# Value products per tile over four column tiles, placed beside each key tile, in a decode attention kernel

## The chip, the cores and the metric

One core of one Trainium2 chip. The metric is the device time of one execution in microseconds (us). Where a text says "span" it means the profiled execution from the first to the last instruction of the core. "Clock" is the share of its full speed that TensorE was granted; the clock records hold 1.0 and 0.5 ("half clock"), and between two changes lie 3.41 us or a multiple of it (3.41 to 40.96 us in the kernel before). A "stop" is idle time of TensorE that ended for no reason that the profile shows; the lines mark it `<-issue`. A run is called slow when it is over 1.5% above the fastest of the same kernel; medians are over all runs.

## The reference, cut to what matters

```python
# A: one decode step of attention, batch 4, 32 query heads on 8 key/value heads, head size 128, window 4096
q = (x @ wq).reshape(B, 1, 32, 128)
k = k_cache[:, :, -4096:, :]; v = v_cache[:, :, -4096:, :]      # each repeated 4 times over the query heads
p = softmax(q @ k^T * 128 ** -0.5)
a = (p @ v).reshape(B, 1, 4096) @ wo
# B: a small gated feed-forward of the same x;   g = sigmoid(sum(x * gate_w))
out = g * a + (1 - g) * b
```

Keys and values of the window are 67 MB of the 81 MB that are read. Everything else is small, so loading is the floor: the 81.01 MB of the page take 191 us at the 425 GB/s of its slices, an estimate.

## The kernel before

The cache is cut into 16 tiles of keys (`k 0..15`) and 16 of values (`v 0..15`), 2 MB each: one batch entry and two heads, called a pair. Two pairs make a set (8 sets). One queue on the sync engine issues all loads in a fixed order; keys have 4 slots and values 5. Per set TensorE transposes the key tiles (KT), multiplies by the queries (SC), exchanges row maxima (SW), transposes the exponentials (PT), sums rows (RS), multiplies by the values (PV), regroups the result (OQ) and at the end projects with `wo` (WO). Each engine is given its instructions in the order of this list:

```python
def _pe_order():
    ...
    for s in range(2, NSET):
        o += [("KT", 2 * s), ("PT", s - 1), ("KT", 2 * s + 1), ("SC", s), ("PV", s - 2), ("SW", s), ("RS", s - 2),
              ("OQ", s - 2)]
        if s == 6:
            o.append(("WO", 0))
    last = NSET - 1
    o += [("PV", last - 1), ("RS", last - 1), ("PT", last), ("RS", last), ("OQ", last - 1)]
    o += [("PVL", 0), ("OQL", 0), ("WO", 2), ("PVL", 1), ("OQL", 1), ("WO", 3)]
```

The value products of a set are 128 matrix products with 8 weight columns, alternating between the two pairs and two column tiles of each pair. "Column tile" is said here of the place that `pos` below gives to a product (0, 32, 64 or 96); its 8 rows of the result begin at that row of the bank. The last set is done pair by pair (PVL), so there only two of the four column tiles are in use:

```python
def pv_mm(s, pair, ch, ev=None, waits=()):
    c0 = 32 * (ch // 2) + 16 * pair + 8 * (ch % 2)
    r = 64 * pair + 32 * (ch % 2)                       # the column tile
    mm(banks[OB][r:r + 8, 0:128], pT[:, s % 2, c0:c0 + 8],
       Vsb[:, (2 * s + pair) % VSLOTS, 128 * ch:128 * ch + 128], ch < 2, ch > 61, ..., pos=(0, r))
...
w = [("PV", (i - VSLOTS) // 2)] if i >= VSLOTS else []   # a value load waits for the whole set that held its slot
...
def _kt_on_act(i, f):                                   # which of 8 blocks of a key tile ScalarE copies back
    return i % 2 == 1 and f % 2 == 1
```

## Time and profile before

| | before |
|---|---|
| timed median (3 runs) | 219.79 us (218.59 to 220.63) |
| span of the profiled run | 216.0 us |
| loads at about 425 GB/s | from 2.4 to 191.7 us, then a gap, last value piece at 202.77 us |
| last set's scores start, last exponentials end | 187.46, 198.92 us |
| TensorE busy, mean clock | 156.3 us (72%), 0.897 |

The part of the page that follows the chain of work back from the last instruction says how much of the span each engine and each line carried:

```profile
PE 40%; DMA 36%; ACT 10%; DVE 7%; issue 4%; SPq 2%; ACTq 0%; DVEq 0%
DMA Ksb<-in_A_k_cache_dram 29%; PE bank L327 26%; PE bank L331 14%; DMA Wbig<-in_A_wq_dram 8%; ACT Ksb L670 7%; ACT pe L693 2%; DVE Ksb L553 2%; DVE pe L585 2%; SPq L251 2%; DVE qblk L577 1%; DVE osb L620 1%; DVE pT L611 1%; DVE osum L656 0%; DVE hmax L604 0%; DVE negmax L606 0%
```

The reader should see that key loads carry 29% and all loads 36% of the chain: in the middle the engines wait for keys, and only the last part is a chain of engines. The prediction shows that part line by line.

### The profile page before, as it was taken

To read this page: it belongs to the slowest core of one execution; us is meant where nothing else is said; L and a number is where in the kernel's file an instruction comes from. 1 tells how busy PE (TensorE), PEld (TensorE's weight loads), DVE (VectorE), ACT (ScalarE), POOL (GpSimd) and SP (SyncE) were. 2 spreads that over 40 slices of the span, in tenths; PEclk is the share of its full clock that TensorE was granted. 3 is DMA by queue.
4 is the path that set the end of the run, shared out by engine and by line. 5 is a ranking of instruction groups with operands and counts; after the bars stand their busy time and mean duration, and the time that the engine had idled before them with its cause. 6 is when DMAs were issued, how large, how long until landed. Compare 5 with 4: busy or idle time off the path is not lost.

```text
span 216.0 us, 5261 instructions
## 1 busy us (share of the span) xinstructions
PE 156.3 (72%) x2398; PEld 109.2 (51%) x2398; DVE 114.0 (53%) x257; ACT 76.9 (36%) x70; POOL 3.4 (2%) x16
## 2 busy tenths in 40 slices
PE   0385917889991057889788788578778599785894
PEld 0382605367261055388277457545763347445751
DVE  3181682787575013569469559346785119561302
ACT  2000313287053015084446618151860720618000
POOL 6000000000000000000000000000000000000000
PEclk9996797999999558969999999799999879999569
DMA  5999999999999999999999999999999999818300
GB/s 200 444 425 410 428 426 423 439 429 420 425 396 415 433 431 428 425 428 425 425 428 422 428 434 419 425 425 423 432 428 419 419 425 434 376 58 271 124 0 1
DMA packets 6837, 81.33 MB, mean 377 GB/s; under 512 B 792, under 2 KB 800, under 8 KB 2336
## 3 DMA queue, kind: packets, MB, share of 16 engines
q1 hardware_dynamic: 6816, 81.01, 89.4%
q8 instruction: 18, 0.29, 0.6%
q14 instruction: 3, 0.02, 0.0%
HBM read 81.01 MB, written 0.00 MB: 375 GB/s over the span
## 4 chain that ended last, share of the span: by engine, by line
PE 40%; DMA 36%; ACT 10%; DVE 7%; issue 4%; SPq 2%; ACTq 0%; DVEq 0%
DMA Ksb<-in_A_k_cache_dram 29%; PE bank L327 26%; PE bank L331 14%; DMA Wbig<-in_A_wq_dram 8%; ACT Ksb L670 7%; ACT pe L693 2%; DVE Ksb L553 2%; DVE pe L585 2%; SPq L251 2%; DVE qblk L577 1%; DVE osb L620 1%; DVE pT L611 1%; DVE osum L656 0%; DVE hmax L604 0%; DVE negmax L606 0%
## 5 line engine op out<-in xcount | busy, mean ns | idle before, releaser
L331 PE MATMUL bank<-identf,Ksb 128*128 128x128 f32 x512 | 72.9, 304 | 28.1 <-DMA Ksb<-in_A_k_cache_dram 21.1
L331 PEld LDWEIGHTS bank<-identf,Ksb 128*128 128x128 f32 x512 | 65.3, 158 | 33.3 <-issue 12.9
L553 DVE COPY Ksb<-bank 128x1024 bf16<-128x1024 bf16 x96 | 61.5, 685 | 36.4 <-PE bank L331 36.1
L693 ACT ACTIVATE pe<-sc,negmax 64x2048 bf16<-64x2048 bf16 x16 | 41.6, 2601 | 52.8 <-DVE negmax L606 52.6
L670 ACT ACTIVATE Ksb<-bank 128x1024 bf16<-128x1024 bf16 x32 | 31.5, 1023 | 48.1 <-PE bank L331 48.0
L327 PE MATMUL bank<-Ksb,qblk 128*8 128x512 bf16 x256 | 30.8, 622 | 8.9 <-ACT Ksb L670 8.9
L595 DVE TENSOR_SCALAR_CACHE_REDUCE sc<-bank 128x512 bf16<-128x512 f32 x32 | 22.1, 692 | 21.3 <-PE bank L327 21.3
L327 PEld LDWEIGHTS bank<-Vsb,pT 128*8 128x8 bf16 x1024 | 19.1, 91 | 6.3 <-issue 6.3
L327 PE MATMUL bank<-Vsb,pT 128*8 128x128 bf16 x1024 | 20.8, 228 | 1.6 <-issue 1.1
L327 PEld LDWEIGHTS bank<-Ksb,qblk 128*8 128x8 bf16 x256 | 4.6, 88 | 29.2 <-DVE sc L595 13.4
L327 PE MATMUL bank<-sel,pe 128*128 128x32 bf16 x256 | 8.1, 178 | 6.7 <-ACT pe L693 6.6
L611 DVE CAST pT<-bank 128x512 bf16<-128x512 f32 x16 | 10.3, 682 | 3.3 <-PE bank L327 3.3
L327 PEld LDWEIGHTS bank<-sel,pe 128*128 128x128 bf16 x256 | 7.3, 97 | 8.2 <-DVE Ksb L553 5.9
L327 PE MATMUL bank<-Wbig,oq 128*4 128x512 bf16 x32 | 10.7, 500 | 0.7 <-DVE oq L640 0.7
L327 PE MATMUL bank<-oneh,osb 128*32 128x4 bf16 (+1 forms) x144 | 3.3, 176 | 7.0 <-DVE osb L620 5.0
L620 DVE TENSOR_SCALAR osb<-bank,recip 128x128 bf16<-128x128 f32 (+1 forms) x9 | 3.2, 351 | 8.7 <-PE bank L327 8.5
L327 PEld LDWEIGHTS bank<-oneh,osb 128*32 128x32 bf16 (+1 forms) x144 | 2.4, 115 | 8.1 <-DVE osb L620 6.0
L327 PEld LDWEIGHTS bank<-Wbig,oq 128*4 128x4 bf16 x32 | 3.0, 101 | 5.9 <-issue 3.5
L681 ACT ACTIVATE ge<-bank 4x1 f32<-4x1 f32 x2 | 0.2, 152 | 14.5 <-PE bank L327 14.5
L327 PE MATMUL bank<-Wbig,xT 128*4 128x512 bf16 x32 | 3.6, 625 | 2.2 <-DMA Wbig<-in_A_wq_dram 2.2
L604 DVE TENSOR_TENSOR hmax<-bank,rowmax 128x1 f32<-128x1 f32 x8 | 1.2, 156 | 7.4 <-PE bank L327 7.4
L585 DVE MEMSET pe<- 64x2048 bf16 x2 | 3.5, 1765 | 1.2 <-issue 1.2
(52 smaller groups left out, 48.3 us busy)
## 6 DMA issues: line engine op xcount, KB each, us to landing
Ksb<-in_A_k_cache_dram SPq DMA_DIRECT2D x16, 2048.0 KB, 25.3
Vsb<-in_A_v_cache_dram SPq DMA_DIRECT2D x15, 2048.0 KB, 25.5
Wbig<-in_A_wq_dram SPq DMA_DIRECT2D x1, 4096.0 KB, 16.3
Wbig<-in_A_wo_dram SPq DMA_DIRECT2D x1, 4096.0 KB, 31.0
Vsb<-in_A_v_cache_dram SPq DMA_DIRECT2D x4, 512.0 KB, 6.6
Vsb<-in_B_W_gate_dram SPq DMA_DIRECT2D x1, 1792.0 KB, 24.1
Vsb<-in_B_W_up_dram SPq DMA_DIRECT2D x1, 1792.0 KB, 33.3
Vsb<-in_B_W_down_dram SPq DMA_DIRECT2D x1, 1792.0 KB, 41.2
```

What stands on the lines that cost most here:

```text
L251: E.op(lambda: e.dma_start(dst, src), ev=ev, waits=waits, ctr=ctr)
L327: E.op(lambda: t.matmul(out_, lhsT, rhs, start=start, stop=stop, tile_position=pos, skip_group_check=True), ev=ev, waits=waits)
L331: E.op(lambda: t.transpose(out_, in_, idn), ev=ev, waits=waits)
L553: E.op(lambda: v.tensor_copy(kt_dst(i, f), bankb[tr(key)]), ev=("E",) + key, waits=[key])
L577: E.op(lambda r=r, u=u, b=b: v.tensor_copy(qv[r, b, n, :, :, :, u], src[r, :, :, b, :]), ev=("E",) + key if lastop else None, waits=[key, ...
L585: E.op(lambda n=n: v.memset(pev[64 * n:64 * n + 64, :, 1 - n], 0.0), ev=("PEZ",) if n else None, waits=[("QT", 1)])
L595: E.op(lambda: v.tensor_scalar(sc[:, 512 * f:512 * f + 512], banks[scb(key)], 1.0, None, op0=ALU.mult, op1=ALU.max, accum_out=mx4[:, f:f + ...
L604: E.op(lambda: v.tensor_tensor(hmax[:, :], banks[tr(key)][:, 0:1], rowmax[:, :], ALU.max), ev=("E",) + key, waits=[key])
L611: E.op(lambda: v.tensor_copy(pT[:, s % 2, 512 * f:512 * f + 512], banks[tr(key)]), ev=("E",) + key, waits=[key] + ([("PV", s - 2)] if s >= ...
L620: E.op(lambda: v.tensor_scalar(osb[r, s % 2, :], banks[OB][r, 0:128], recip[r, s % 2:s % 2 + 1], None, op0=ALU.mult), ev=ev, waits=waits)
L670: E.op(lambda: a.activation(kt_dst(i, f), bankb[tr(key)], ACTF.Copy), ev=("E",) + key, waits=[key])
L693: E.op(lambda r=r, n=n: a.activation(pev[r, :, n], sc[r, :], ACTF.Exp, bias=negmax[r, s % 2:s % 2 + 1], scale=SCALE, accum_out=rowsum[r, s ...
```

## The change

Its intent: do the value products one tile at a time, so that they fit into gaps beside each key tile, so that a value slot comes free per tile, and so that all four column tiles are used to the end. The core of the diff:

```diff
     for s in range(2, NSET):
-        o += [("KT", 2 * s), ("PT", s - 1), ("KT", 2 * s + 1), ("SC", s), ("PV", s - 2), ("SW", s), ("RS", s - 2),
-              ("OQ", s - 2)]
+        i = 2 * s
+        o += [("KT", i), ("OQ", i - 4), ("PT", s - 1), ("RS", s - 1)]
+        o += [("PV", i - 3), ("KT", i + 1)] if s < NSET - 1 else [("KT", i + 1), ("PV", i - 3)]
+        o += [("SC", s), ("OQ", i - 3), ("PV", i - 2), ("SW", s)]
         if s == 6:
             o.append(("WO", 0))
...
+    i = NPAIR - 4
+    o += [("OQ", i), ("PV", i + 1), ("PT", NSET - 1), ("OQ", i + 1), ("RS", NSET - 1), ("PV", i + 2), ("OQ", i + 2)]
+    o += [("WO", 1), ("PV", i + 3), ("OQ", i + 3), ("WO", 2)]
...
 # loads: "k 14, v 11, k 15, v 12 ..." becomes "k 14, k 15, v 11, v 12 ..."
...
-    return i % 2 == 1 and f % 2 == 1
+    return i % 2 == 1 and f in (1, 3, 6)
...
-                w = [("PV", (i - VSLOTS) // 2)] if i >= VSLOTS else []
+                w = [("PV", i - VSLOTS)] if i >= VSLOTS else []
...
+        def PV(i):
+            s, pair = i // 2, i % 2
...
+                r = 32 * (ch % 4)
+                c0 = 32 * (ch // 2) + 16 * pair + 8 * (ch % 2)
+                mm(banks[OB][r:r + 8, 0:128], pT[:, s % 2, c0:c0 + 8], Vsb[:, i % VSLOTS, 128 * ch:128 * ch + 128],
+                   ch < 4, ch > 59, ev=("PV", i) if ch == 63 else None, waits=w, pos=(0, r))
```

Row sums now need two products per set (one per pair), and norm, regrouping and its copy are done 16 times instead of 9. The rest of the diff is masks and names.

## The prediction

The packets in it are the 16 KiB ones of the instruction queue; the page of the kernel before lists 18. Two of its figures are estimates of its author: 27 ns for a value product over four column tiles at half clock, about half of the 56 ns over two (64 in 3.58 us), and 0.22 us for a projection at full clock, half of its 0.43 at half clock (8 in 3.51 us).

> **What bounds the kernel now.** I read the page's slices first, then the transfer queue's own timeline, then TensorE's timeline of the last third, then the chain that ended last. The slices (5.4 us each):
>
> ```profile
> PEclk9996797999999558969999999799999879999569
> DMA  5999999999999999999999999999999999818300
> GB/s 200 444 425 410 428 426 423 439 429 420 425 396 415 433 431 428 425 428 425 425 428 422 428 434 419 425 425 423 432 428 419 419 425 434 376 58 271 124 0 1
> ```
>
> To the reader: for 34 slices the DMA engines are full at about 425 GB/s, so up to about 190 us nothing that the engines do is worth anything unless it holds up a load. Then comes a hole (58 GB/s), a second piece of traffic, and about 13 us with no transfer at all. The gain is in those last slices. The hole has an owner in the queue's timeline (start us, us, queue, line, transfer, count):
>
> ```profile
> 150.50 0.61 SPq L251 DMA_DIRECT2D Ksb<-in_A_k_cache_dram  x1
> 151.14 45.04 SPq L251 DMA_DIRECT2D Vsb<-in_A_v_cache_dram  x7
> ```
>
> The last seven issues are value tiles 12, 13, 14 and the four pieces of 15; they stretch to 196 us because tile 15 may not be issued before its slot is given back. The landing records of the trace say: tile 14 complete at 191.70, pieces of tile 15 at 197.35 to 202.77. In the full stretch one 2 MB tile lands every 4.89 us, so without that wait tile 15 would be there at 191.7 + 4.9 = 196.6. But TensorE comes to tile 15's products only at 207.5, so the late load is not what ends the kernel. TensorE's timeline (start us, us, operation, count, idle before) shows what does:
>
> ```profile
> 166.30 1.98 PE L327 MATMUL bank<-Vsb,pT 128*8 128x128 bf16 x128
> ...
> 171.61 0.20 PE L327 MATMUL bank<-oneh,osb 128*32 128x4 bf16 x2 [2.02 <-issue]
> ...
> 172.01 4.88 PE L327 MATMUL bank<-Wbig,oq 128*4 128x512 bf16 x15
> 176.83 3.89 PE L331 MATMUL bank<-identf,Ksb 128*128 128x128 f32 x32
> 180.66 1.16 PE L327 MATMUL bank<-sel,pe 128*128 128x32 bf16 x32
> 181.85 4.36 PE L331 MATMUL bank<-identf,Ksb 128*128 128x128 f32 x32
> 187.46 3.85 PE L327 MATMUL bank<-Ksb,qblk 128*8 128x512 bf16 x32 [1.25 <-ACT Ksb L670]
> ```
>
> Key tile 14 landed at 167.27 and 15 at 177.04, yet their transposes start at 176.83 and 181.85: from 167 us TensorE is behind the loads, not ahead of them. The debt is the half output projection (16 products) with a 2.02 us stop before it. From there on a serial chain runs to the end; its pieces (start us, us, what):
>
> ```profile
> 193.63 2.61 ACT pe L693
> ...
> 196.31 2.61 ACT pe L693 x2
> ...
> 199.61 1.29 DVE pT L611 x2
> ...
> 201.05 3.60 PE bank L327 x64
> ...
> 205.79 3.51 PE bank L327 x35
> 209.30 0.07 issue
> 209.37 1.12 PE bank L327 x33
> ```
>
> That is: both exponentials of the last set, copy of the transposed weights (done at 200.9), 64 value products in 3.6 us, norm and regroup, 8 projections in 3.5 us, the last value products, and 5.5 us of fixed tail from 210.5 to 216.0.
>
> [...]128 value products over four column tiles take 1.98 us (15 ns each); 64 over the two tiles of one pair take 3.58 us at half clock (56 ns). [...]The clock records agree: 0.5 from 171.6 to 175.0, right after the 2.02 us stop, and from 198.9 to 209.1, after the wait for the exponentials. [...]packets that landed at 89.94, 152.93 and 170.14 are each followed 1.2 to 1.5 us later by the end of a TensorE stop of 0.94, 1.15 and 2.02 us that nothing else explains, each after a burst of 128 value products (256 instructions in 2 us). That link is an inference.[...]
>
> **The change part by part.**
> *Value products per tile.* The count stays (1024). Each tile now uses four column tiles instead of two, so a burst is 64 products of about 15 ns, 1.0 us. In the middle this moves work, no more. At the end it shortens: 64 x 56 ns = 3.6 us becomes 64 x 27 ns = 1.75 us at half clock, 1.0 us at full.
> *Additional small work.* Regroup products go from 9 x 16 = 144 to 16 x 16 = 256: 7 additional groups x 0.33 us = 2.3 us. Row sums take two products per set: 8 x 0.36 us = 2.9 us. VectorE gains 7 norms x 0.35 us and 7 copies x 0.19 us, together 3.8 us. All but the last two sets' share (about 0.7 + 0.7 us on TensorE) lies under the loads.
> *Key copies.* ScalarE's share of an odd tile falls from 4 to 3 (1.02 us each), and the last copy goes to VectorE (0.69). Its four took 3.8 us in the set at 158.7; now 5 x 0.65 = 3.2 on VectorE beside 3 x 1.0 on ScalarE. About 0.6 us sooner per set, where the copies bound.
> *Slots given back per tile.* Tile 15 waits for tile 10's products (about 167 us) instead of set 5's (193). The stream should end near 196.6. Alone that is worth nothing now, but it is needed once TensorE is earlier.
> *Last key load one place earlier.* Tile 15 of keys at 172.2 instead of 177.0; value tile 11 at 177.0 instead.
>
> Working from key tile 13, which the loads fix at 157.5 in both kernels: transposes to 161.1, copies to about 161.9, scores (3.85) to 165.9, regroup 0.33, 64 value products 1.0, maximum swap: 167.4. Before, the projections came at 171.6, after 0.7 us of waiting for a norm, the regroup and the stop. Now they start at 167.4. With bursts of 64 between transposes I expect no stop and so full clock: 16 x 0.22 = 3.5 us, to 171.0. Key tile 14: VectorE copies all eight, 8 x 0.64 = 5.1, to 176.6; regroup copy 0.2, two weight copies 1.28, reciprocal 0.16, to 178.2; five copies of tile 15, 3.2, to 181.5. That is the old pace (copies start at 177.52, scores at 187.46), as the copies bound it. Value products of tile 11 lie in this gap, scores start at 181.9 (before 187.46) and end at 185.7. Regroup and tile 12's products 1.35, norm, maximum: 187.7. Two exponentials 5.3: 193.0 (before 198.9). Transposition and copies 2.0: 195.0. TensorE idles some 3.7 us meanwhile, so I expect half clock. Tile 14's products, partly beside the copies: 196.3. Norm, regroup, copy 1.1: 197.4. Eight projections 8 x 0.43 = 3.4: 200.8. Tile 15's products at half clock, partly overlapped, 1.4: 202.2. Fixed tail 5.5, of which the last eight projections might be 1.6 longer at half clock: 207.7 to 209.3. I take a span of 207.9.
>
> The timed median is 219.79 against a span of 216.0, so 3.8 us lie outside; 207.9 + 3.8 = 211.7, and I set 211.5.
>
> **The rivals.**
> *The stream becomes the bound.* If TensorE were faster than I work out, the last piece lands at 196.6, and 16 products, 0.3 us, and the 5.5 us tail give 202.5, timed 206.3. For it: the tail at full clock saves 2 to 3 us. Against it: the exponentials alone end near 193, and there follow 64 products, a norm and eight projections. It is the floor.
> *The stops stay.* TensorE gets 128 more products (112 regroup, 16 in row sums, each of which the profile counts as two)[...]. If a stop of 2 us falls before the projections again, with half clock after it (1.5 us), 3.5 us of the gain go: timed 215.
> *The gain is hidden anyway or the small work eats it.* If TensorE were bound in the middle, 5.2 us of it would delay every set. Against it: TensorE waited 9.80 us for keys at 77.8 and 2.47 us at 137.7, so there is slack. If half of it counted, 214.
> *VectorE becomes the bound.* It has 8 more key copies and 3.8 us of small work, 9 us in all on 114 of 216; between loads it is idle almost half of the time. Only tiles 14 and 15 are tight, and that is in the sum.
>
> **Range and chances.** The sum's uncertain terms are the clock at the end (about 3 us), one stop (2 to 3.5), and run-to-run spread of the timed runs (218.59 to 220.63, so 1). Together 208.0 to 215.0. Two per cent faster is below 215.4; that fails only if a stop and a slow tail come together, or a wait appears that I do not see. Faster 0.91, same 0.08, slower 0.01.
>
> **What would show it.** Right: no hole in the GB/s row before about 196 us; the last value piece lands near 197; projections start near 167.5 at a clock of 1.0; scores of the last set start near 182; exponentials end near 193; 64 value products take 1.0 to 1.8 us at the end. Wrong: a stop over 1 us without a releaser between 160 and 172, the second-last key tile's transposes starting later than 173, a wait of TensorE for a value tile before the last, or a hole in the stream in the middle.

## The result, and the profile after

| | before | after |
|---|---|---|
| timed median, same rounds (4 runs each) | 219.19 us | 213.14 us (211.58 to 213.74) |
| ratio after/before, 95% interval | | 0.971 (0.963 to 0.979) |
| span of the profiled run | 216.0 | 209.9 |
| set 6: scores start | 162.64 | 165.00 |
| half projection starts | 171.63 | 169.97 |
| key tile 14: transposes start | 176.83 | 173.51 |
| set 7: scores start | 187.46 | 184.19 |
| last exponentials end | 198.92 | 195.03 |
| last value piece lands | 202.77 | 197.56 |

Ratios are the mean time of one kernel's fast runs over that of the other's of the same rounds, so not quite the ratio of the medians. By these runs the kernel is 2.9% faster. Run again it was 2.3% faster (0.977, 0.971 to 0.983), an interval that reaches past 0.98: that it is faster is clear in both, that it is over 2% faster only in the first. The profiled run of the changed kernel is also its fastest; its four spans are 209.9, 211.1, 212.0 and 211.7 us.

The slices of the span after the change (5.2 us each):

```profile
PEclk9997976999999955997999799859975999998569
DMA  5999999999999999999999999999999999998200
GB/s 206 419 456 400 419 433 419 434 437 417 428 395 408 440 422 425 434 425 428 418 434 418 428 428 425 436 409 426 425 431 422 428 431 425 425 418 353 81 0 4
```

The hole in the loads is gone. They run full through slice 36 and end in slice 38. The queue's timeline (start us, us, queue, line, transfer, count) shows that nothing holds the last value loads up any more. The queue is through with them at 172 us, where before it stood until 196:

```profile
149.61 22.80 SPq L254 DMA_DIRECT2D Vsb<-in_A_v_cache_dram  x8
```

TensorE's timeline (start us, us, operation, count, idle before and what ended it) for the same steps as in the prediction:

```profile
155.53 1.01 PE L330 MATMUL bank<-sel,pe 128*128 128x32 bf16 x32 [2.01 <-ACT pe L660]
156.38 0.99 PE L330 MATMUL bank<-rowsum,wsum 128*128 128x1 f32 x4
157.30 1.88 PE L330 MATMUL bank<-Vsb,pT 128*8 128x128 bf16 x64
159.11 5.11 PE L334 MATMUL bank<-identf,Ksb 128*128 128x128 f32 x32
165.00 3.85 PE L330 MATMUL bank<-Ksb,qblk 128*8 128x512 bf16 x32 [0.78 <-DVE Ksb L533]
...
169.97 3.62 PE L330 MATMUL bank<-Wbig,oq 128*4 128x512 bf16 x16
173.51 3.89 PE L334 MATMUL bank<-identf,Ksb 128*128 128x128 f32 x32
...
184.19 3.85 PE L330 MATMUL bank<-Ksb,qblk 128*8 128x512 bf16 x32
...
192.53 1.14 PE L330 MATMUL bank<-Vsb,pT 128*8 128x128 bf16 x40 [2.30 <-issue]
...
197.25 1.91 PE L330 MATMUL bank<-Vsb,pT 128*8 128x128 bf16 x64
```

The same key tile and scores in the kernel before:

```profile
157.62 3.75 PE L331 MATMUL bank<-identf,Ksb 128*128 128x128 f32 x32 [0.65 <-DVE Ksb L553]
162.64 3.85 PE L327 MATMUL bank<-Ksb,qblk 128*8 128x512 bf16 x32 [1.27 <-ACT Ksb L670]
```

The half projection now takes 3.62 us and no stop stands before it. The odd key tile 13, however, landed at 157.53 and its transposes only start at 159.11 and take 5.11 us, so the scores of set 6 are 2.4 us later than before. A stop of 2.30 us has turned up in the value products of tile 13, where TensorE waits for the exponentials anyway. Laid side by side, the steps of the profiled runs account for the whole gain: scores of set 6 come later (+2.4); from there to the projections it is shorter (8.99 to 4.97, -4.0); projections (5.20 to 3.54, -1.7); key tiles 14 and 15 (10.63 to 10.68, 0); scores to exponentials (11.46 to 10.84, -0.6); the rest (17.1 to 14.9, -2.2). The sum is -6.1, and 216.0 - 209.9 is 6.1. Of the -4.0, 2.02 us are the stop that stood before the projections, and the -1.7 is the half clock that followed it; whether the new order removed them is a question for the experiments (x7_before_shifted).

Why is set 6 late? The chain that ended last says it. First its shares (engines, then lines):

```profile
PE 48%; DMA 25%; ACT 13%; DVE 9%; issue 2%; SPq 2%; ACTq 0%; DVEq 0%
PE bank L330 32%; DMA Ksb<-in_A_k_cache_dram 17%; PE bank L334 17%; ACT pe L660 13%; DMA Wbig<-in_A_wq_dram 8%; DVE Ksb L533 4%; DVE pe L565 2%; SPq L254 2%; DVE qblk L557 1%; DVE osb L600 1%; DVE negmax L586 0%; DVE osum L623 0%; DVE hmax L584 0%; DVE oq L607 0%; ACTq L95 0%
```

Key loads went from 29% to 17% of the chain. The rest of its middle is a loop of engines, shown here for one turn, from the scores of set 5 to the scores of set 6 (start us, us, what):

```profile
144.44 4.96 PE bank L330 x105
...
150.06 2.69 ACT pe L660 x2
...
152.77 2.62 ACT pe L660 x2
...
155.53 3.65 PE bank L330 x100
159.18 5.05 PE bank L334 x32
...
164.25 0.70 DVE Ksb L533
...
165.00 8.58 PE bank L330 x125
```

Read it as a circle: scores, value products and maximum (4.96); two exponentials (5.3); transposition, row sums and 64 value products (3.65); transposes of the odd key tile (5.05); the last copy (0.70); and the next scores. With 0.9 us of norm, maximum and hand-overs it is 20.56 us per set, while the loads bring a set's four tiles in 4 x 4.89 = 19.56 us. So the changed kernel falls behind the loads by 1.0 us per set wherever the circle is that long. The 3.65 us piece contains the new row sums and value products, at half clock: the clock records are 0.5 from 155.1 to 162.0, after a wait of 2.01 us for the exponentials. Two turns earlier (scores at 104.36 to scores at 123.84) the clock was 1.0 in that piece and it took 2.44 us; that turn took 19.48, with the transposes of its odd key tile at half clock (5.29). So the half clock is part of the length: the turn of 20.56 has 6.8 us of it, the turn of 19.48 has 3.4. In x5_act_four below one turn of this order ran wholly at 1.0 (scores at 84.26 to scores at 102.68); it took 18.42 us, less than the loads' 19.56, with 0.5 us more wait for copies in it.

### The profile page after: what moved, and what is told of

Read it like the earlier page. It is cut to its first block, busy times and chain, and to the rows that moved or that the text cites.

```text
span 209.9 us, 5524 instructions
## 1 busy us (share of the span) xinstructions
PE 157.9 (75%) x2526; PEld 112.2 (53%) x2526; DVE 121.5 (58%) x279; ACT 69.8 (33%) x62; POOL 4.3 (2%) x19
## 4 chain that ended last, share of the span: by engine, by line
PE 48%; DMA 25%; ACT 13%; DVE 9%; issue 2%; SPq 2%; ACTq 0%; DVEq 0%
PE bank L330 32%; DMA Ksb<-in_A_k_cache_dram 17%; PE bank L334 17%; ACT pe L660 13%; DMA Wbig<-in_A_wq_dram 8%; DVE Ksb L533 4%; DVE pe L565 2%; SPq L254 2%; DVE qblk L557 1%; DVE osb L600 1%; DVE negmax L586 0%; DVE osum L623 0%; DVE hmax L584 0%; DVE oq L607 0%; ACTq L95 0%
## 5 line engine op out<-in xcount | busy, mean ns | idle before, releaser
L533 DVE COPY Ksb<-bank 128x1024 bf16<-128x1024 bf16 x104 | 66.3, 685 | 33.6 <-PE bank L334 32.8
L334 PEld LDWEIGHTS bank<-identf,Ksb 128*128 128x128 f32 x512 | 66.4, 160 | 26.8 <-issue 10.2
L637 ACT ACTIVATE Ksb<-bank 128x1024 bf16<-128x1024 bf16 x24 | 24.3, 1023 | 55.1 <-PE bank L334 55.1
L330 PEld LDWEIGHTS bank<-Vsb,pT 128*8 128x8 bf16 x1024 | 17.9, 96 | 3.1 <-issue 2.7
L600 DVE TENSOR_SCALAR osb<-bank,recip 128x128 bf16<-128x128 f32 x16 | 5.6, 351 | 16.0 <-PE bank L330 15.5
L330 PE MATMUL bank<-Wbig,oq 128*4 128x512 bf16 x32 | 8.6, 425 | 0.7 <-DVE oq L607 0.7
L330 PEld LDWEIGHTS bank<-oneh,osb 128*32 128x32 bf16 x256 | 4.6, 115 | 7.0 <-issue 4.0
L330 PE MATMUL bank<-oneh,osb 128*32 128x2 bf16 x256 | 5.3, 176 | 1.3 <-DVE osb L600 1.3
L330 PE MATMUL bank<-rowsum,wsum 128*128 128x1 f32 x32 | 6.0, 292 | 0.0
L330 PEld LDWEIGHTS bank<-rowsum,wsum 128*128 128x128 f32 x32 | 5.5, 242 | 0.1
```

The costliest lines, as they stand in the source:

```text
L330: E.op(lambda: t.matmul(out_, lhsT, rhs, start=start, stop=stop, tile_position=pos, skip_group_check=True), ev=ev, waits=waits)
L334: E.op(lambda: t.transpose(out_, in_, idn), ev=ev, waits=waits)
L533: E.op(lambda: v.tensor_copy(kt_dst(i, f), bankb[tr(key)]), ev=("E",) + key, waits=[key])
L600: E.op(lambda: v.tensor_scalar(osb[:, i % 2, :], banks[OB][:, 0:128], recip[:, i % 4:i % 4 + 1], None, op0=ALU.mult), ev=("NORM", i), wait ...
L637: E.op(lambda: a.activation(kt_dst(i, f), bankb[tr(key)], ACTF.Copy), ev=("E",) + key, waits=[key])
```

## The experiments

The theory before them was the loop: the value products of the previous odd tile stand between the exponentials and the odd key tile, on the circle, and TensorE idles 2.0 us just before. The rivals: the half clock comes with any wait, or the end alone decides. "Ratio" is always to the kernel before, of the same rounds; the changed kernel had 0.971, and later 0.977.

### Value products moved off the loop (x1_pv_early)

```diff
-        o += [("KT", i), ("OQ", i - 4), ("PT", s - 1), ("RS", s - 1)]
-        o += [("PV", i - 3), ("KT", i + 1)] if s < NSET - 1 else [("KT", i + 1), ("PV", i - 3)]
+        o += [("KT", i), ("OQ", i - 4)]
+        o += [("PV", i - 3), ("PT", s - 1), ("RS", s - 1), ("KT", i + 1)] if s < NSET - 1 else [
+            ("PT", s - 1), ("RS", s - 1), ("KT", i + 1), ("PV", i - 3)]
```

> Changed kernel with one move in sets 2 to 6: the 64 value products of the previous odd tile stand before the transposition of the exponentials instead of after it. Theory (the loop): from set 3 on the changed kernel is bound by the loop exponentials, transposition, row sums, value products, transposes of the odd key tile, scores, and these 64 products (1.1 us, 1.9 at half clock) lie on it, while TensorE idles 2.0 us just before. Moved into that idle time they leave the loop: scores of set 6 start 1 to 2.5 us earlier than the 165.0 of the changed kernel, the odd key tile's transposes start within 0.3 us of its landing (157.5), the idle time before the transposition falls from 2.0 to about 1.0, and the span goes from 209.9 to about 208.4; timed ratio to the kernel before about 0.964 (the changed kernel 0.971). Rival 1 (the lateness comes from the half clock that any wait brings): clock 0.5 stays at 155 to 162, and scores of set 6 start at 165 as now. Rival 2 (the end is bound by the tail alone): scores of set 6 come earlier, the span does not move.

Measured: median 208.99 us (208.88 to 210.19), ratio 0.959 (0.953 to 0.965), span 207.0. TensorE's timeline:

```profile
157.53 3.75 PE L335 MATMUL bank<-identf,Ksb 128*128 128x128 f32 x32 [0.88 <-DMA Ksb<-in_A_k_cache_dram]
162.06 3.85 PE L331 MATMUL bank<-Ksb,qblk 128*8 128x512 bf16 x32 [0.78 <-DVE Ksb L534]
```

The odd key tile is waited for again: 0.88 us for a load; as in the kernel before, its transposes start within 0.2 us of its landing. They take 3.75 us, and scores of set 6 start 2.9 us earlier than in the changed kernel. Rival 2 falls (the span moved by the same 2.9 us). Rival 1 expected the half clock and the late scores to stay, and they did not (clock 1.0 from 142 to 190); but as both went together, this run alone does not part the products from the clock. Three other runs do: x2, x8 and x10 have the products off the loop and key tile 13 at half clock, and scores of set 6 start at 163.63, 163.62 and 163.66. So about 1.4 of the 2.9 us come from the move itself and 1.6 from the clock. This is the best kernel and beats both. Its four runs (208.88 to 210.19) lie below all eight runs of the changed kernel (211.58 to 214.65), which are of other calls, and below the four of x4_key_old_place (211.77 to 214.40), which is of the same call and differs from the changed kernel by a load that turns out not to matter.

### Row sums moved as well (x2_pv_early_rs_late)

Against x1_pv_early:

```diff
-            ("PT", s - 1), ("RS", s - 1), ("KT", i + 1)
+            ("PT", s - 1), ("KT", i + 1), ("RS", s - 1)
```

> As x1_pv_early, and the row sums (0.6 us, 1.0 at half clock) stand behind the odd key tile's transposes, where TensorE waits 0.78 us for copies in any case. Theory (the loop): another 0.6 us goes off the loop wherever the loop still binds; where the loads bind again it is worth nothing until set 7, where the row sums of set 6 (0.6 us) stood before the last key tile: span about 207.8. Rival: no difference to x1_pv_early, as vector copies of the even tile bound the last set.

Measured: median 211.08 us (208.5 to 212.16), ratio 0.962 (0.950 to 0.974), span 209.0. Less on the loop, and yet no better. The profile says why:

```profile
157.49 5.35 PE L335 MATMUL bank<-identf,Ksb 128*128 128x128 f32 x32 [1.92 <-DMA Ksb<-in_A_k_cache_dram]
```

TensorE is now 1.92 us ahead of key tile 13, idles, and the clock is 0.5 from 158.4 to 161.8. The transposes take 5.35 us instead of 3.75. So x1's rival 1 was half right: not every wait brought the half clock. The 1.92 us before this tile were followed by it, and the tile took 1.6 us longer; the 0.88 us in x1 were not. In the 3.4 us before 158.4 TensorE was busy for 1.50 us here; in x1 the two stretches from 152.4 to 159.2 had 2.30 and 2.53, and the clock stayed at 1.0. (From 158.4 to 161.8 TensorE did nothing but transposes, and the clock was 1.0 after that.) Scores of set 6 start at 163.63.

### Two column tiles at the end (x3_two_tiles_end)

```diff
-                r = 32 * (ch % 4)
+                two = i >= NPAIR - 2
+                r = 32 * (ch % 2 if two and ch > 3 else ch % 4)
...
-                   ch < 4, ch > 59, ...
+                   ch < 4, (ch > 61 or ch in (2, 3)) if two else ch > 59, ...
```

> Changed kernel, but the value products of tiles 14 and 15 alternate between two column tiles, as at the end of the kernel before (the first four still open all four). Result stays right. Theory: the four column tiles are worth about 1.7 us for tile 14 and 0.5 to 1.5 us for tile 15: at half clock the 64 products of tile 14 take 3.5 us instead of 1.9, span 212 to 213, timed ratio about 0.983. Rival: products of small tiles are bound by their issue, not by column tiles: no change, 209.9.

Measured: median 216.98 us, ratio 0.993 (0.985 to 1.000), span 215.0. The value products of tiles 14 and 15:

```profile
199.13 3.47 PE L330 MATMUL bank<-Vsb,pT 128*8 128x128 bf16 x64
...
206.73 2.84 PE L330 MATMUL bank<-Vsb,pT 128*8 128x128 bf16 x60
```

Tile 14 takes 3.47 us instead of 1.91. From the scores of set 7 to the end it is 28.9 us (186.07 to 215.0), against 25.7 in the changed kernel (184.19 to 209.9) and 26.9 when that was run again (186.05 to 212.9). The four column tiles are worth 2 to 3 us at the end. The span missed its expectation by 2 us, but scores of set 7 were already 1.9 us late, before the edit can count; they start as late (186.05) when the unedited changed kernel is run again.

### Last key load in its old place (x4_key_old_place); slots by set (x6_slots_by_set); four copies on ScalarE (x5_act_four)

Three parts of the change undone, one at a time:

```diff
-            o[-1:] = [("k", NPAIR - 1)] + o[-1:]                                # first kernel
+            o.append(("k", NPAIR - 1))
-                w = [("PV", i - VSLOTS)] if i >= VSLOTS else []                  # second kernel
+                w = [("PV", (i - VSLOTS) // 2 * 2 + 1)] if i >= VSLOTS else []
-    return i % 2 == 1 and f in (1, 3, 6)                                         # third kernel
+    return i % 2 == 1 and f % 2 == 1
```

> Changed kernel with the last key load back in its old place, behind value tile 11. Key tile 15 then lands at about 177.1 instead of 172.2. Its transposes start at 179.6 in the changed kernel, so theory says no difference: span 209.9 within 0.4, ratio 0.971. Rival: the earlier place shields the last key tile from being late, and without it the last scores start later by up to 1 us.

Measured (x4_key_old_place): median 213.32 us, ratio 0.977 (0.969 to 0.985), span 212.7. The span missed its expectation by 2.4 us; where is seen from the steps. Key tile 15 landed at 177.18 and its transposes started at 182.41, so nothing waited for it. From the scores of set 5 (147.25), before the two kernels differ in anything that could count, to the end it is 65.5 us; in the changed kernel it is also 65.5 (144.44 to 209.9). The place of the last key load is worth nothing here.

> Changed kernel, but a value slot counts as given back only when both tiles of its set are done, as before. The last value tile then waits for the products of tile 11 (184.2) instead of tile 10 (169.9). The loads before it keep the engines full to about 191.7, so theory says no difference: no hole in the stream, span 209.9 within the 2 us in which runs of the changed kernel differ, ratio 0.971. Rival, which the prediction held: giving slots back per tile is needed for the stream to end near 197; without it the last piece lands 3 us or more later.

Measured (x6_slots_by_set): median 213.78 us, ratio 0.976 (0.970 to 0.983), span 212.1. The last piece landed at 198.31, within 0.8 us of the changed kernel's 197.56, and the stream has no hole. Giving slots back per tile is not needed: with the new order tile 11's products are done at 185 us, and the queue has issued its last piece at 187.9, before the loads in flight run dry (191.7). It is the order that closed the hole. The prediction's "it is needed once TensorE is earlier" falls.

> Changed kernel with ScalarE copying four blocks of every odd key tile as before (1, 3, 5, 7) instead of three. Theory: the wait between the odd tile's last transpose and the first score product grows from 0.78 back to about 1.25 us, which lies on the loop; each set of the loop is 0.4 to 0.5 us longer, and the end 0.5 to 1.5 us later: span 210.5 to 212, ratio about 0.975. Rival: the copies are hidden, no change in the wait.

Measured (x5_act_four): median 214.44 us, ratio 0.972 (0.961 to 0.983; only two of its four runs count as fast, and its profiled run counts as slow). The wait before the scores of set 6:

```profile
166.31 3.90 PE L330 MATMUL bank<-Ksb,qblk 128*8 128x512 bf16 x32 [1.27 <-ACT Ksb L637]
```

It is 1.27 us instead of 0.78, as expected, and waits of 1.25 and 1.27 us stand before the scores of sets 2 to 5 as well. So the split of the copies is worth 0.5 us of wait per turn of the loop. In the time that is not clear of noise.

### The kernel before, with its instructions shifted (x7_before_shifted)

```diff
             bk = bankb[tr(("XT",))]
+            for q in list(range(4)) * 8:      # the same small transposes 8 times more
+                tp(bk[:, 4 * q:4 * q + 4], xsb[0:4, q:q + 509:4], identb[0:4, 0:4], ...)
```

> Kernel before with 32 additional small transposes (the same results written again) early, where TensorE waits for the query weights. Nothing else changes, but every later instruction stands 64 places later in TensorE's stream. Theory[...]: the stop of 2.02 us before the half output projection in the kernel before[...] shifted by 64 places it lies at another point of the work: the projections start near 169.7 instead of 171.6 and run at clock 1.0 (3.6 us instead of 4.9), key tile 14's transposes start near 173.4 instead of 176.8, span about 212.5, or a stop of the same kind turns up elsewhere. Rival: the stop belongs to the place (the wait for the norm, the traffic) and stays at 169.6 to 171.6; span 216.

Measured: median 218.74 us, ratio 0.995 (0.985 to 1.005): the same. The profiled run was the quickest of the four (215.83; the others 218.49 to 219.80). Its profile:

```profile
148.71 0.25 PE L327 MATMUL bank<-rowsum,wsum 128*128 128x1 f32 x1
152.17 0.16 PE L327 MATMUL bank<-rowsum,wsum 128*128 128x1 f32 x1 [3.21 <-issue]
...
172.45 3.40 PE L327 MATMUL bank<-Wbig,oq 128*4 128x512 bf16 x15
```

The stop of 2.02 us before the projections is gone, they run at full clock, and a stop of 3.21 us stands a set earlier, between two row sums. The program is the same but for the position in TensorE's stream. So in these two kernels the stops go with the position in the instruction stream (2.02 us before the shift, 3.21 us elsewhere after it). The other runs agree: the changed kernel, its second run and x1 to x6 have the same number of TensorE instructions before tile 13's products, and all eight profiles have a stop (1.58 to 2.56 us) at the same place in them, with 40 products still to come. A packet of 16 KiB on the instruction queue landed at 150.94, and the stop ended 1.23 us later. The time did not follow, as the new stop delays the next key tiles: scores of set 6 start at 164.78 instead of 162.64. From there to the end it is 49.3 us, in the kernel before 53.4 and in the changed kernel 44.9. So of the 8.5 us that the changed kernel gains behind that point, about half (4.0) goes with a stop, and the half clock after it, that a mere shift also takes away from there; the other 4.4 are left for the new order and the four column tiles. Why a stop follows some packets and not others is not shown by any run.

### Work that keeps TensorE busy (x8_warm, x9_warm_shifted, x10_pv_early_shifted, x11_filled)

The kernel with the products off the loop, and 16 idle products while the last exponentials run:

```diff
-    o += [("OQ", i), ("PV", i + 1), ("PT", NSET - 1), ...
+    o += [("OQ", i), ("WARM", 12), ("PV", i + 1), ("WARM", 4), ("PT", NSET - 1), ...
+        def WARM(n):
+            for _ in range(n):
+                mm(banks[SCB[0]], Ksb[:, 0, 0:128], Ksb[:, 0, 0:512], True, True, waits=[("E", "SC", NSET - 1, 3)])
```

> x1_pv_early with 16 idle products (128x512, results not used, into a score bank that is free by then): 12 before and 4 behind the value products of tile 13, while the last exponentials run. Theory: in x1 the clock is 0.5 from 190.0 to 200.2 because TensorE idles while it waits for the last exponentials; kept busy it stays at 1.0, tile 14's products take 1.0 us instead of 1.9, the row sums 0.6 instead of 1.0, the eight projections 1.8 instead of 2.7 and more, so TensorE would be 2.5 us earlier, and then the last value piece (landing at 198.2 in x1) plus 0.3 plus the tail of 5.5 sets the end: span about 204.3, timed ratio about 0.946. Rival 1: the filling work delays the transposition of the last set (12 + 4 products and the stop of 1.8 us exceed the wait) and eats the gain: span 206 to 208. Rival 2: the clock falls anyway.

Measured (x8_warm): median 211.12 us (209.64 to 212.33), ratio 0.964 (0.955 to 0.973), span 209.4. The expectation failed. The row sums took 0.61 us instead of 1.01, but:

```profile
196.88 1.44 PE L331 MATMUL bank<-Vsb,pT 128*8 128x128 bf16 x45 [0.99 <-issue]
```

A stop fell into tile 14's products, on the chain, and the clock was 0.5 from 196.0, although TensorE had been busy for 2.73 of the 3.4 us before. Rival 2 is what happened. From the last scores to the end it is 26.6 us, against 25.8 in x1. With 72 tiny products added early, which move the later instructions by 144 places:

```diff
+        if s == 2:
+            o.insert(-1, ("PAD", 72))         # 72 products of 128x32, before key tile 5
```

> x8_warm with 72 additional tiny products early, where TensorE waits for key tile 5; they move every later instruction 144 places back. In x8 a stop of 0.99 us fell into tile 14's products, on the chain, and the clock fell at 196.0. Theory: the stop moves into the regrouping of tile 14 or vanishes; with it gone the clock stays 1.0 longer, tile 14's products take 1.0 us and from the start of the last set's scores to the end it is 23 to 24.5 us (x1_pv_early 25.8, x8_warm 26.6); span about 205 to 206, timed ratio about 0.95. Rival: the clock falls at 196 whatever is done[...]; 25.5 us or more from scores to end.

```profile
197.86 1.07 PE L333 MATMUL bank<-Vsb,pT 128*8 128x128 bf16 x64
```

Measured (x9_warm_shifted): median 211.06 us, ratio 0.964 (0.958 to 0.970), span 208.4. Here the local expectation held: no stop, clock 1.0 from 182.5 to the end, tile 14 in 1.07 us, and 23.5 us from the last scores (184.87) to the end. But the clock had been 0.5 for key tile 13 (158.6 to 162.0) and key tile 15 (179.1 to 182.5), so the scores started late and the time is no better than without it. The shift alone, without filling work:

> x1_pv_early with the same 72 tiny products and no filling work. In x1 a stop of 1.84 us cuts tile 13's products, inside the wait for the last exponentials. Theory: the stop moves by 144 places, out of tile 13's products; the transposition of the last set starts as before relative to the scores (10.9 us after them), as the exponentials set it; timed ratio 0.959 within 0.005. Rival: the stop stays at tile 13's products.

Measured (x10_pv_early_shifted): median 211.22 us (210.28 to 213.04), ratio 0.967 (0.959 to 0.976), span 209.2. The stop left tile 13's products, and the transposition of the last set started 11.1 us after the scores (182.84, 193.98). The ratio missed its band: key tile 13 was waited for by 2.60 us and transposed at half clock in 5.35 us, as in the run with the row sums moved. And with six more products of zeros in the wait before each odd key tile of sets 3 to 6:

```diff
+        if 3 <= s < NSET - 1:
+            o.insert(-1, ("FILL", s, 6))      # zer x Wbig, 128x512, into a free score bank
```

> x9_warm_shifted (value products before the transposition, filling work at the end[...]), and six products of a zero block (128x512, into a score bank that is free then) before the odd key tile in sets 3 to 6; 48 instead of 72 tiny products early[...]. Theory: in x9 and x10 TensorE is ahead of the loads, waits 2.6 us for key tile 13 and gets the half clock for it, so that its transposes take 5.35 us instead of 3.75; with six products (1.3 us) in that wait the clock stays 1.0, scores of set 6 start at 162.0 to 162.8 instead of 164.1, and with the 23.5 us from the last scores to the end of x9 the span is 205 to 206, timed ratio 0.945 to 0.955. Rival: products of zeros, or 1.3 us of them, do not hold the clock: scores of set 6 at 164, ratio 0.964 as x9.

Measured (x11_filled, 6 runs): median 210.86 us (210.0 to 211.6), ratio 0.969 (0.964 to 0.974), span 208.6.

```profile
161.87 3.85 PE L337 MATMUL bank<-Ksb,qblk 128*8 128x512 bf16 x32 [0.78 <-DVE Ksb L553]
...
198.04 0.29 PE L337 MATMUL bank<-oneh,osb 128*32 128x2 bf16 x5 [1.87 <-issue]
```

The first half came out as expected: the clock is 1.0 from 82.8 to 198.8 and scores of set 6 start at 161.87. The second did not: a stop of 1.87 us landed in the regrouping of tile 14, on the chain, with half clock after it, and from the last scores to the end it took 27.6 us (181.04 to 208.6) instead of 23.5. A kernel with both halves would be near 181.0 + 23.5 = 204.5 us of span; that is an estimate from two runs and was not reached.

### The changed kernel once more (after_again)

> The changed kernel once more, beside the two, to see how far its own runs lie apart on one chip: timed ratio 0.971 within 0.006; the period of the scores in the middle 19.4 us where the clock is 1.0 after the exponentials' wait and 20.6 where it is 0.5.

Measured: median 213.73 us (212.76 to 214.65), ratio 0.977 (0.971 to 0.983), span 212.9, mean clock 0.84. From scores to scores it is 20.8, 20.6, 20.6 and 20.5 us (84.37, 105.14, 125.76, 146.31, 166.83), each with the row sums at half clock (0.99 us). So the changed kernel often runs the long circle from the start; the run that was profiled first had two short turns of 19.5. In this run the half clock begins at 95.52, 116.00, 136.48 and 156.96, each time 20.48 us later, which is six times 3.41: with turns of 20.5 to 20.8 us, each of these turns met the half clock near the same point again.

## Why the prediction was right, and where not

It said 211.5 us in 208 to 215; 213.14 was measured, 2.9% faster. Its signs: no hole, the last piece, and no stop and full clock at the projections came as written; 64 products at the end took 1.91 us, just over the 1.8; projections, last scores and end of the exponentials came 2.0 to 2.5 us later than written, and one sign of being wrong came true, key tile 14's transposes starting at 173.51, later than 173. Step by step:

- **The bound, and the path from the projections on,** were right. Its steps came out within 0.3 us: projections to last scores 14.2 us (worked out 14.5), scores to the end of the exponentials 10.84 (11.1), exponentials to the end 14.9 (14.9). In the last, two errors cancel: the working left the row sums (1.01 us) out here too, so the eight projections start 5.3 us after the exponentials instead of 4.4, and what follows takes 9.6 instead of 10.5. That is luck.
- **"Working from key tile 13, which the loads fix at 157.5 in both kernels"** is the step that failed. With it fails "All but the last two sets' share [...] lies under the loads". The working did not count the row sums and the 64 value products that stand between the transposition and that tile, nor any half clock there. They lie on a circle of 20.56 us, with 6.8 us of half clock in it, longer than the loads' 19.56. The transposes began at 159.11 and at half clock; scores of set 6 started 3.0 us after the 162.0 that the working implies. Moving the products away brought 162.06, about half of it by the clock. The third rival, small work that counts in the middle, was the right one to fear, and the reason given against it (waits for keys of 9.80 and 2.47 us) was a slack of the old order.
- **No stop before the projections, and full clock there**: right (3.62 us against 3.5), but the reason given, shorter bursts, is not shown. A stop of 2.30 us came back in a burst of 64, tile 13's products, and the shifted kernels show that its place goes with the position (tile 13's products hold 1.84 us of stop in x1_pv_early; in x10_pv_early_shifted, 144 places later, all 64 take 1.1 us). That this one lay in a wait for the exponentials, and none before the projections, was luck; it is worth 3.7 us between the two profiles (2.02 of stop, 1.7 of clock).
- **Four column tiles at the end**: 1.91 us at half clock for a worked-out 1.75; two tiles 3.47 for 3.6. The run with two tiles shows 2 to 3 us in all.
- **The slots**: the last piece at 197.56 for 196.6, right; that the per-tile release is what it needs, wrong. **The key load's place**: right that it brings nothing that TensorE uses. **The copies**: 0.5 us per turn for 0.6.
- **From span to time**: 3.8 us were added, the difference of a median and one profile. Within one run it is about 1.8; the rest was that the profiled run before was a quick one (217.82 us). Set against the median span of the changed kernel, 211.4, the working was 3.5 us short, and the 3.8 us hid about half of that. So the time (1.6 us short) came closer than its parts, by luck.

What stays open: why TensorE stops at one place of its stream and not at another, and how much of the 2 us between the best kernel and its shifted variants is the phase of the clock. They run the same order of work and differ mostly in which key tile got the half clock.

## What to carry to other kernels

When loads bound a kernel, work moved "under the loads" is free only if the longest circle of dependences per round stays shorter than the loads' period (here it was 20.56 us against 19.56); add up that circle, at half clock too, before moving anything onto it, and put movable work where the engine waits in any case. Shortening the circle below the period is not free either: the engine then idles, and here the next tile ran at half clock (x2_pv_early_rs_late: 1.92 us of wait, then 5.35 us instead of 3.75). Stops of 0.94 to 3.21 us whose place moved with the position in the stream make single profiles of such variants differ, so compare step by step from a common point rather than by the total.

## What the traces show of the stops and the clock

- In three kernels TensorE stops of 0.94 to 3.21 us end 1.23 to 1.50 us after a 16 KiB packet of the instruction queue has landed: in the kernel before, packets at 89.94, 152.93 and 170.14 and stops that end at 91.37, 154.16 and 171.61; in the changed kernel 191.03 and 192.53; in x7_before_shifted 150.94 and 152.17. Most packets have no such stop after them: the kernel before has 18 packets and three stops over 0.9 us. The stops were elsewhere when 64 (x7_before_shifted) or 144 (x10_pv_early_shifted) instructions were added early.
- With products of zeros in the wait before the odd key tiles the clock stayed at 1.0 from 82.8 to 198.8 us (x11_filled), where the same order without them had 0.5 from 117.7 to 124.5 and from 158.6 to 162.0 (x9_warm_shifted). In x9 a stretch (175.7 to 179.1) in which TensorE was busy for 3.09 us, over half of it with regrouping, transposition by 32 columns and row sums, was followed by 0.5.
- The traces have value products between the sixth and seventh of eight projections that stand before them in program order, by the starts that the profile records (202.44 and 202.86 us in the changed kernel).
- Four column tiles, for 128-column products with 8 weight columns: 64 in 1.91 us at half clock against 3.47 over two tiles (x3_two_tiles_end).
